# The last token tile's product in two column groups, each summed and stored when its own matmuls end

## The chip, the cores and the metric

The kernel runs on one core of a Trainium2 chip. The metric is the device time of one execution in microseconds (us). A run gives several executions; times of two kernels are compared within rounds taken on the same chip.

Names in the profiles: PE is TensorE (matmuls) and PEld its weight loads, DVE is VectorE, ACT ScalarE, POOL GpSimd and SP SyncE; a `q` after a name marks the engine's sequencer, which waits and issues DMAs. SBUF is the working memory; PSUM, in banks, is where matmuls sum up. A DMA has *landed* when the last update of its semaphore arrives.

A profile's *span* runs from its first to its last instruction. It is about 1.7 us shorter than the device time of the same execution (172.957 against 174.68 us for the kernel before).

## The reference, cut to what matters

Each of 2048 tokens (448 features) goes through a linear-attention block and a mixer-plus-MLP block in parallel. Both end in a matrix product, and their sum leaves the kernel:

```python
# x: 2048 x 448;  xn = layernorm(x)
# ... attention output o (2048 x 448), MLP hidden h3 (2048 x 1792), x1 = xn + mixer ...
out = x + (o @ wo) + (x1 + h3 @ w4)
```

The tokens are worked in 16 tiles of 128. For one tile, `h3 @ w4` takes 14 matmuls with a contraction of 128, and `o @ wo` takes 4 (here with padding to 128). All 18 accumulate in one PSUM bank. Then VectorE adds `xs`, which is `x + x1` of that tile, and the result is stored.

## The kernel before

Every operation is recorded first; waits are then worked out from what it reads and writes. Two rules of that matter here. SBUF is tracked in small pieces, but PSUM by whole bank: a matmul that writes a bank waits for every earlier reader on another engine of any column of that bank. And waits are placed mainly between different engines; in the last tile no matmul waits for an earlier matmul, so PE's own instructions simply follow each other.

```python
def _keys(self, ap):
    ...
    if psum:
        lo = (ap.offset * esz) % row_bytes
        hi = lo + esz + sum(step * (num - 1) for step, num in list(ap.ap)[1:]) * esz
        return [(name, b) for b in range(lo // 2048, (hi - 1) // 2048 + 1)]   # whole banks
    ...

def play(e, eng):                      # one engine's instructions
    mine = []
    for fn, todo, src, dma in self.stream[eng]:
        for f, i in todo:
            e.wait_ge(...)
        ins = fn(e)
        ...
    for f in mine:                     # at the end: wait for this engine's own stores
        if f not in self.marked:
            e.wait_ge(get(f), 16)
```

The end of the kernel:

```python
def x_sum(i):
    R.ew(pool, "tensor_tensor", xs[:, i % 2, :], xn[:, i, 0:D], xtok[:, i, :], op=ALU.add)

def fin_bank(i):
    return (0 if i > 13 else 4) + i % 2

def fin_full(i):
    g, j = divmod(i, 4)
    b = banks[fin_bank(i)]
    x_sum(i)
    for fc in range(FC):               # FC = 14
        R.mm(b[:, 0:D], h3T[:, g % 2, fc, 128 * j:128 * j + 128], w4[:, fc, :], fc == 0, False)
    for kc in range(KC):               # KC = 4
        R.mm(b[:, 0:D], oT[:, g % 2, kc, 128 * j:128 * j + 128], wo[:, kc, :], False, kc == KC - 1)

# ... all other tiles, in pairs ...
fin_full(14)
fin_out(14)                            # one add of 448 columns
store(14)
fin_full(15)
for h in range(2):
    c = slice(224 * h, 224 * h + 224)
    R.ew(dve, "tensor_tensor", outb[:, 3, c], banks[fin_bank(15)][:, c], xs[:, 1, c], op=ALU.add)
    R.dma(out2d[128 * 15:, c], outb[:, 3, c], "ACT" if h else "SP")
```

So before the change, the last tile is 18 matmuls of 448 columns, then two adds of 224 columns, each with its own store, the first issued by SP, the second by ACT.

The softmax here doesn't subtract the row's maximum and nothing guards it: scores larger than these inputs give would overflow.

## Time and profile before

| | before |
|---|---|
| device time, median of 3 (lowest to highest) | 174.75 us (174.6 to 175.1) |
| span of the profile | 173.0 us |
| PE busy | 168.8 us, 98% of the span |
| first matmul of the last tile | 166.63 us |
| last matmul of the last tile ends | about 170.2 us |
| from the first matmul of the last tile to the end of the span ("the tail") | 6.33 us |

Two lines of the profile's page say who is the bottleneck. The first gives each engine's busy time, its share of the span and its instruction count; the second the shares of the chain that ended last.

```profile
PE 168.8 (98%) x2254; PEld 90.0 (52%) x2254; DVE 114.2 (66%) x263; ACT 84.3 (49%) x99; POOL 88.7 (51%) x123
...
PE 97%; DVE 0%; ACT 0%; issue 0%; DVEq 0%
```

The last lines of that chain in order of time (start, duration, what) show PE without a break until 170.21 us. The chain does not follow a store to its landing, so its end is not the end of the span.

```profile
24.40 145.81 PE bank L200 x1924
170.21 0.02 issue
170.23 0.39 DVE vaug L212
170.62 0.30 DVEq L173
```

The timeline of the end (start, duration, engine, line, operation, out<-in, shape, count, and in brackets the idle time before and who ended it). `w,phik` are the operands of the MLP product, `wo,xnT` of the attention product, and the VectorE output tile goes by the name `vaug`, whose memory it reuses.

```profile
166.63 2.81 PE L200 MATMUL bank<-w,phik 128*128 128x448 bf16 x14
...
169.28 0.92 PE L200 MATMUL bank<-wo,xnT 128*128 128x448 bf16 x4
170.23 0.69 DVE L212 TENSOR_TENSOR vaug<-bank,vaug 128x224 bf16<-128x224 f32 x2 [2.78 <-PE bank L200]
170.95 0.36 ACTq L218 DMA_DIRECT2D out_dram<-vaug  x1
```

What to see: VectorE idles 2.78 us until PE's last matmul is done, then does *both* adds, and only then can ACT issue the last store. The view of DMA issues gives the median time from issue to landing in the last column:

```profile
out_dram<-vaug SPq DMA_DIRECT2D x15, 112.0 KB, 1.9
...
out_dram<-vaug SPq DMA_DIRECT2D x1, 56.0 KB, 1.5
out_dram<-vaug ACTq DMA_DIRECT2D x1, 56.0 KB, 1.6
```

170.95 + 1.6 us is about 172.55; about 0.4 us more pass until the span ends.

### The profile page before, as it was taken

How to read it: one execution, taken by the hardware profiler on the slowest of the kernel's cores; microseconds unless marked ns; L12 is line 12 of the kernel's file. 1: busy time of each engine (PE TensorE's matmuls, PEld its weight loads, DVE VectorE, ACT ScalarE, POOL GpSimd, SP SyncE). 2: the span in 40 equal slices, each digit the busy share in tenths (PEclk: the TensorE clock that was granted, in tenths of full speed). 3: DMA queues.
4: the chain of work that ended last, by engine and by line, in shares of the span. 5: the costliest groups of instructions: out<-in, count | busy, mean ns of one | idle time of the engine just before them, and what ended most of it. 6: DMA issues, size and time to landing. Idle time of an engine off the chain costs nothing.

```text
span 173.0 us, 5182 instructions
## 1 busy us (share of the span) xinstructions
PE 168.8 (98%) x2254; PEld 90.0 (52%) x2254; DVE 114.2 (66%) x263; ACT 84.3 (49%) x99; POOL 88.7 (51%) x123
## 2 busy tenths in 40 slices
PE   7999999999999999999999999999999999999993
PEld 5565576544555554554545555555545545545451
DVE  4999976277999999976678953436407434474711
ACT  3599874988778877947225222224213222224000
POOL 3065570015789999930749388540721705423740
PEclk9999999999999999999999999999999999999999
DMA  5996642129942011043103824035321210311331
GB/s 164 347 216 79 143 90 56 35 46 366 380 151 48 18 30 30 4 55 70 34 0 75 83 61 87 5 84 111 73 51 34 74 44 4 83 34 30 83 107 29
DMA packets 32678, 15.20 MB, mean 88 GB/s; under 512 B 24080, under 2 KB 32016, under 8 KB 32656
## 3 DMA queue, kind: packets, MB, share of 16 engines
q1 hardware_dynamic: 32096, 14.48, 35.2%
q10 hardware_dynamic: 560, 0.40, 0.8%
q8 instruction: 17, 0.28, 0.7%
q14 instruction: 5, 0.04, 0.1%
HBM read 7.14 MB, written 1.84 MB: 52 GB/s over the span
## 4 chain that ended last, share of the span: by engine, by line
PE 97%; DVE 0%; ACT 0%; issue 0%; DVEq 0%
PE bank L200 96%; PE bank L204 1%; ACT xnT L208 0%; DVE vaug L212 0%; DVEq L173 0%; DVE gT L212 0%
## 5 line engine op out<-in xcount | busy, mean ns | idle before, releaser
L208 ACT ACTIVATE phik<-bank 128x1024 bf16<-128x1024 f32 (+1 forms) x44 | 42.3, 984 | 60.3 <-PE bank L200 60.2
L200 PE MATMUL bank<-gT,w 64*128 64x512 bf16 x392 | 50.0, 377 | 0.0
L212 DVE TENSOR_TENSOR vaug<-bank,vaug 128x464 f32<-128x464 f32 (+3 forms) x65 | 32.6, 512 | 23.0 <-PE bank L200 21.4
L200 PE MATMUL bank<-w,phik 64*128 64x448 bf16 (+1 forms) x420 | 45.0, 349 | 0.0
L212 POOL TENSOR_TENSOR xnT<-vaug 128x196 bf16<-128x196 f32 (+1 forms) x32 | 18.0, 585 | 46.4 <-DVE vaug L212 46.4
L200 PEld LDWEIGHTS bank<-w,phik 64*128 64x128 bf16 (+1 forms) x420 | 21.7, 94 | 21.2 <-issue 0.4
L212 POOL TENSOR_TENSOR phik<-phik,rks 128x1792 bf16<-128x1792 bf16 x8 | 25.6, 3212 | 10.4 <-DVE rks L212 10.3
L200 PEld LDWEIGHTS bank<-gT,w 64*128 64x128 bf16 x392 | 17.6, 94 | 17.5 <-ACT phik L208 0.4
L212 POOL TENSOR_TENSOR vaug<-xn,xtok 128x448 f32<-128x448 bf16 x16 | 16.2, 1032 | 0.2 <-DVE vaug L212 0.2
L212 DVE TENSOR_REDUCE ksum<-phik 128x64 f32<-128x1792 bf16 x8 | 16.1, 2011 | 0.0
L212 DVE RECIPROCAL vaug<-bank 128x16 f32<-128x16 f32 x16 | 4.1, 256 | 18.0 <-PE bank L200 18.0
L200 PE MATMUL bank<-xnT,wpq 64*128 64x512 bf16 x112 | 14.7, 376 | 0.0
L200 PE MATMUL bank<-wv,xnT 64*128 64x448 bf16 x112 | 13.9, 351 | 0.1
L200 PE MATMUL bank<-wo,xnT 64*128 64x448 bf16 (+1 forms) x106 | 13.4, 349 | 0.0
L200 PE MATMUL bank<-xnT,w 64*128 64x512 bf16 (+2 forms) x168 | 13.3, 306 | 0.0
L200 PE MATMUL bank<-w,hT 64*128 64x448 bf16 x112 | 13.2, 349 | 0.0
L200 PE MATMUL bank<-wpk,xnT 64*128 64x448 bf16 x112 | 13.2, 349 | 0.0
L212 POOL TENSOR_TENSOR rs<-mv,mhalf 128x1 f32<-128x1 f32 (+2 forms) x16 | 10.8, 674 | 1.3
L212 DVE TENSOR_TENSOR xn<-bank,xn 128x512 bf16<-128x512 f32 (+1 forms) x16 | 9.2, 619 | 3.1 <-PE bank L200 3.1
L212 DVE BATCH_NORM_STATS2 st<-xtok 128x6 f32<-128x448 bf16 x16 | 9.8, 612 | 0.0
L212 POOL TENSOR_SCALAR mv<-mv 128x1 f32<-128x1 f32 (+2 forms) x16 | 3.8, 238 | 11.3 <-DVE mv L212 10.9
L212 DVE BATCH_NORM_STATS2 st<-xn 128x6 f32<-128x448 bf16 x16 | 9.2, 577 | 0.0
(67 smaller groups left out, 173.4 us busy)
## 6 DMA issues: line engine op xcount, KB each, us to landing
w<-in_B_w_dram SPq DMA_DIRECT2D x2, 896.0 KB, 5.9
out_dram<-vaug SPq DMA_DIRECT2D x15, 112.0 KB, 1.9
w<-in_B_w_dram SPq DMA_DIRECT2D x1, 1568.0 KB, 11.1
xtok<-in_A_x_dram SPq DMA_DIRECT2D x2, 448.0 KB, 5.7
xtok<-in_A_x_dram SPq DMA_DIRECT2D x2, 224.0 KB, 4.4
w<-in_B_w_dram SPq DMA_DIRECT2D x2, 224.0 KB, 4.6
wo<-in_A_wo_dram SPq DMA_DIRECT2D x2, 224.0 KB, 7.0
xtok<-in_A_x_dram SPq DMA_DIRECT2D x3, 112.0 KB, 2.6
```

Source lines behind the costliest of these rows:

```text
L200: self.op("PE", lambda e: e.matmul(out, lhsT, rhs, start=start, stop=stop, skip_group_check=True), [out], [lhsT, rhs], tile=self._tile(lhsT))
L204: self.op("PE", lambda e: e.transpose(out, in_, ident), [out], [in_, ident], tile=self._tile(in_))
L208: self.op("ACT", lambda e: e.activation(out, in_, func, **kw), [out], [in_] + aps)
L212: self.op(eng, lambda e: getattr(e, name)(out, *args, **kw), [out], aps)
```

## The change

The intent: let VectorE sum and store most of the last tile while PE still works on the rest, so that only a narrow add and a small store remain after PE's last matmul. The 448 columns are done as a group of 336 in bank 1, then a group of 112 in bank 2. `x_sum` moves out of `fin_full`; POOL's order of work stays the same.

```diff
-        def fin_full(i):
+        def fin_full(i, c0=0, c1=D, b=None):
             g, j = divmod(i, 4)
-            b = banks[fin_bank(i)]
-            x_sum(i)
+            b = banks[fin_bank(i) if b is None else b]
             for fc in range(FC):
-                R.mm(b[:, 0:D], h3T[...], w4[:, fc, :], fc == 0, False)
+                R.mm(b[:, c0:c1], h3T[...], w4[:, fc, c0:c1], fc == 0, False)
             for kc in range(KC):
-                R.mm(b[:, 0:D], oT[...], wo[:, kc, :], False, kc == KC - 1)
+                R.mm(b[:, c0:c1], oT[...], wo[:, kc, c0:c1], False, kc == KC - 1)
 ... (cut)
+        x_sum(14)
         fin_full(14)
         fin_out(14)
         store(14)
-        fin_full(15)
-        for h in range(2):
-            c = slice(224 * h, 224 * h + 224)
-            R.ew(dve, "tensor_tensor", outb[:, 3, c], banks[fin_bank(15)][:, c], xs[:, 1, c], op=ALU.add)
-            R.dma(out2d[128 * 15:, c], outb[:, 3, c], "ACT" if h else "SP")
+        x_sum(15)
+        for c0, c1, bk, eng in ((0, 336, 1, "SP"), (336, D, 2, "ACT")):
+            fin_full(15, c0, c1, bk)
+            R.ew(dve, "tensor_tensor", outb[:, 3, c0:c1], banks[bk][:, c0:c1], xs[:, 1, c0:c1], op=ALU.add)
+            R.dma(out2d[128 * 15:, c0:c1], outb[:, 3, c0:c1], eng)
```

More of the change, by code (lines that the diff above doesn't have):

```diff
@@ L731, in fin_bank @@
             return (0 if i > 13 else 4) + i % 2
-        def fin_full(i):
+        def fin_full(i, c0=0, c1=D, b=None):
             g, j = divmod(i, 4)
-            b = banks[fin_bank(i)]
-            x_sum(i)
+            b = banks[fin_bank(i) if b is None else b]
             for fc in range(FC):
-                R.mm(b[:, 0:D], h3T[:, g % 2, fc, 128 * j:128 * j + 128], w4[:, fc, :], fc == 0, False)
+                R.mm(b[:, c0:c1], h3T[:, g % 2, fc, 128 * j:128 * j + 128], w4[:, fc, c0:c1], fc == 0, False)
             for kc in range(KC):
-                R.mm(b[:, 0:D], oT[:, g % 2, kc, 128 * j:128 * j + 128], wo[:, kc, :], False, kc == KC - 1)
+                R.mm(b[:, c0:c1], oT[:, g % 2, kc, 128 * j:128 * j + 128], wo[:, kc, c0:c1], False, kc == KC - 1)
         def fin_pair(i):
```

## The prediction

> # Prediction
>
> **What bounds the kernel now.** TensorE: the page gives PE 98% of the 173.0 us span, and the chain of waits is 97% PE, unbroken from 24.4 to 170.2 us. The change touches only what comes after 166.6 us, the end of that chain. Read from the timeline:
>
> - The last tile's 18 matmuls (128x128 weights, 448 columns) run from 166.63 to about 170.20 us. From (3.57 - 0.353)/17 they start 189 ns apart, each shown 353 ns long.
> - Then VectorE does two adds of 128x224, 170.23 to 170.92 us (385 ns each, overlapping by some 80 ns). It waited 2.8 us for PE before.
> - ACT's queue issues the second half's store at 170.95; it lands about 1.6 us later (DMA issues, 56 KB); the span ends at 173.0.
>
> So 2.75 us of tail follow PE: 0.7 us of adds, 1.6 us of store, about 0.4 us of end.
>
> **What the change does.** Same products, now 18 matmuls of 336 columns into one bank, then 18 of 112 into another; 18 more matmuls and weight loads.
>
> 1. PE. [...] 189 ns at 448 columns, and about 28 ns per pair of row halves at 62 columns, where each matmul has its own weight load too, so loads hid even there. [...] 18 x (142.5 + 49.2) = 3.45 us against 18 x 189.2 = 3.41 us. PE ends about 0.045 us later. [...]
> 2. First add and store (336 columns): a line through the trace's two lengths (385 ns at 224, 613 ns at 448) gives about 500 ns, from about 169.4 to 169.9 us; the store (SP queue) lands about 171.6, hidden behind the second group and the last store.
> 3. Last add: 112 columns, about 270 ns by the same line, about 170.28 to 170.55 instead of 170.92: -0.37 us, PE's +0.045 included.
> 4. Last store: 28 KB in 224-byte rows instead of 56 KB in 448-byte rows. A full-row store took about 1.67 us, the half-row one 1.6; another halving is worth about -0.05 us. [...]
>
> Nothing else is on the path: POOL's sums of both tiles are done by 166.1 us and keep their order; the second group's bank was last read by the GELU of an earlier pair, long before.
>
> **Sum.** -0.37 - 0.05 = about -0.4 us: 174.75 to 174.33 us (-0.25%), inside the 2% band. Range 174.0 to 174.75. Chances: faster by over 2% 0.01, within 2% 0.98, slower by over 2% 0.01.
>
> **What the profile should show.** PE instructions 2254 to 2272. Matmul starts about 142 ns apart in the first group, 49 in the second; PE ends at 170.2 to 170.3 us. A 336-column add inside PE's busy time; a 112-column add of about 270 ns as VectorE's only work after PE. The last store issued by ACT at about 170.6; span about 172.5 us.
>
> **What would make it wrong.** 128-row weight loads that don't hide behind 49 ns matmuls [...]; 224-byte-row stores slower than 448-byte ones; a wait at the start of the second group; run-to-run spread (174.6 to 175.1) of the size of the gain.

The 142.5 ns at 336 columns and 49.2 ns at 112 in point 1 are my estimates; the line through the two spacings of the trace of before, 189.2 ns at 448 columns and 28 ns a pair at 62, gives 142.4 and 48.9 ns.

## The result, and the profile after

| | before | after |
|---|---|---|
| device time, median of 6 | 174.89 us (174.6 to 175.1) | 174.53 us (174.3 to 174.8) |
| ratio, with its 95% interval | | 0.9981 (0.9966 to 0.9995) |
| span of the profile | 173.0 us | 172.7 us |
| PE instructions | 2254 | 2272 |
| tail | 6.33 us | 5.86 us |

Before was timed again in the same rounds as after, so its median is of 6 here and of 3 above. A ratio is the mean time of one kernel's runs over the mean of the other's of the same rounds, so it is not quite the ratio of the medians. The time fell by 0.36 us in the medians, 0.2%, with an interval that just excludes no change.

PE's line of the page after the change:

```profile
PE 168.5 (98%) x2272; PEld 91.3 (53%) x2272; DVE 114.2 (66%) x263; ACT 84.4 (49%) x99; POOL 88.8 (51%) x123
```

The timeline of its end, in the columns of before:

```profile
166.83 2.16 PE L200 MATMUL bank<-w,phik 128*128 128x336 bf16 x14
...
168.83 0.73 PE L200 MATMUL bank<-wo,xnT 128*128 128x336 bf16 x4
...
169.40 0.85 PE L200 MATMUL bank<-w,phik 128*128 128x112 bf16 x14
169.60 0.51 DVE L212 TENSOR_TENSOR vaug<-bank,vaug 128x336 bf16<-128x336 f32 x1 [1.94 <-PE bank L200]
...
170.08 0.36 PE L200 MATMUL bank<-wo,xnT 128*128 128x112 bf16 x4
170.48 0.27 DVE L212 TENSOR_TENSOR vaug<-bank,vaug 128x112 bf16<-128x112 f32 x1 [0.38 <-PE bank L200]
170.79 0.36 ACTq L218 DMA_DIRECT2D out_dram<-vaug  x1
```

And its DMA issues:

```profile
out_dram<-vaug SPq DMA_DIRECT2D x1, 84.0 KB, 1.6
out_dram<-vaug ACTq DMA_DIRECT2D x1, 28.0 KB, 1.5
```

The 336-column add now runs inside PE's busy time, and one add of 0.27 us follows PE instead of a pair of 0.69 us. The matmuls of the second group start 49 ns apart: 14 of them fill 0.85 us, the last one shown 213 ns long, so (0.85 - 0.213)/13 = 49 ns.

**Cutting the tail into steps.** The runs of one kernel spread by half a microsecond and more, which is as much as the effect. But that spread comes before the last tile: its first matmul starts anywhere from 166.48 to 168.08 us in the profiles. From there on the profiles repeat to about 0.02 us. So the theory is tested on the tail. The trace's semaphore events and instruction starts cut it into five steps that add up to it:

| step, us | before | after | difference |
|---|---|---|---|
| PE: first matmul of the tile to the last group's sum ready | 3.583 | 3.627 | +0.044 |
| VectorE: from there to the last add done | 0.723 | 0.308 | -0.415 |
| hand-over to the last store's issue | 0.021 | 0.022 | 0 |
| last store: issue to landing | 1.598 | 1.493 | -0.105 |
| landing to the end of the span | 0.405 | 0.405 | 0 |
| tail | 6.330 | 5.855 | -0.475 |

The tail gained 0.475 us; in this pair of profiles 0.20 us of that was lost again by a later start of the last tile (166.83 against 166.63). The difference arises in one place, in code that the change doesn't touch: up to 81.3 us PE was 0.08 us ahead of before, from 81.5 us on it was 0.21 us behind. The view of the waits, for 81 to 82.5 us of after, has a pause of the weight loads there (total, times, longest) that the same window of before has not:

```profile
PEld bank L200 <- issue: 0.6, 1, 0.6
```

"issue" means that the profile shows nothing to wait for. The semaphore events show it: PE waits there for four transposing DMAs that feed the next token group, the last of which landed at 81.19 us in before and at 81.45 in after. In the other profiles it landed between 81.0 and 82.7 us.

### The profile page after: what moved, and what is told of

It is laid out like the page before. It is cut to its first block, busy times and chain, and to the rows that moved or that the text cites. A ratio compares the mean times of both kernels' runs of the same rounds, so it can differ in the third digit from the quotient of the medians.

```text
span 172.7 us, 5218 instructions
## 1 busy us (share of the span) xinstructions
PE 168.5 (98%) x2272; PEld 91.3 (53%) x2272; DVE 114.2 (66%) x263; ACT 84.4 (49%) x99; POOL 88.8 (51%) x123
## 4 chain that ended last, share of the span: by engine, by line
PE 95%; DVE 2%; issue 1%; ACT 0%
PE bank L200 94%; PE bank L204 1%; DVE vaug L212 1%; DVE st L212 1%; ACT xnT L208 0%; DVE xn L212 0%; DVE mv L212 0%; DVE gT L212 0%; DVE rs L212 0%; DVE epsb L212 0%
## 5 line engine op out<-in xcount | busy, mean ns | idle before, releaser
L200 PE MATMUL bank<-w,phik 64*128 64x448 bf16 (+3 forms) x434 | 45.2, 343 | 0.0
L200 PEld LDWEIGHTS bank<-w,phik 64*128 64x128 bf16 (+1 forms) x434 | 22.9, 94 | 20.3 <-issue 0.4
L200 PE MATMUL bank<-wo,xnT 64*128 64x448 bf16 (+3 forms) x110 | 13.6, 343 | 0.0
L212 POOL TENSOR_SCALAR g_tok<-xn,rs 128x512 bf16<-128x512 bf16 x12 | 9.1, 776 | 0.3
(67 smaller groups left out, 173.0 us busy)
```

Source lines behind the costliest of these rows:

```text
L200: self.op("PE", lambda e: e.matmul(out, lhsT, rhs, start=start, stop=stop, skip_group_check=True), [out], [lhsT, rhs], tile=self._tile(lhsT))
L212: self.op(eng, lambda e: getattr(e, name)(out, *args, **kw), [out], aps)
```

## The experiments

Twelve runs, five rounds each (one is the changed kernel unedited, one repeats e2); all gave correct results. **The theory**: the gain is a shorter add after PE and a smaller last store, less a small cost on PE; it needs the second bank; nothing else moved. **Rivals**: that it is chance; that the finer adds and stores alone bring it; that it comes from any early store, whichever group is last; that the bank doesn't matter.

All tails and their steps, read as above ("sum" is PE's step, "add" VectorE's, "store" from issue to landing, "end" from landing to the end of the span; hand-over is 0.02 in all):

| kernel | sum | add | store | end | tail | ratio to before (95%) |
|---|---|---|---|---|---|---|
| before | 3.583 | 0.723 | 1.598 | 0.405 | 6.330 | |
| after | 3.627 | 0.308 | 1.493 | 0.405 | 5.855 | 0.9981 (0.9966 to 0.9995) |
| e0_again | 3.626 | 0.310 | 1.480 | 0.410 | 5.847 | 0.9984 (0.9946 to 1.0022) |
| e1_onebank | 4.403 | 0.309 | 1.481 | 0.405 | 6.620 | 1.0032 (0.9998 to 1.0065) |
| e2_addsonly | 3.582 | 0.723 | 1.626 | 0.410 | 6.363 | 1.0027 (0.9987 to 1.0067) |
| e2_repeat | 3.581 | 0.724 | 1.610 | 0.405 | 6.342 | 1.0014 (0.9988 to 1.0040) |
| e3_order | 3.626 | 0.542 | 1.666 | 0.415 | 6.271 | 0.9998 (0.9966 to 1.0029) |
| e4_c64 | 3.628 | 0.259 | 1.602 | 0.404 | 5.914 | 0.9977 (0.9956 to 0.9997) |
| e5_half | 3.628 | 0.425 | 1.576 | 0.409 | 6.059 | 0.9987 (0.9968 to 1.0006) |
| e6_swap | 3.627 | 0.310 | 1.451 | 0.498 | 5.902 | 0.9976 (0.9951 to 1.0001) |
| e7_c32 | 3.783 | 0.284 | 1.732 | 0.404 | 6.223 | 0.9994 (0.9974 to 1.0013) |
| e8_three | 3.671 | 0.258 | 1.446 | 0.405 | 5.801 | 0.9985 (0.9958 to 1.0012) |
| e9_swaprev | 3.627 | 0.309 | 1.455 | 0.416 | 5.824 | 0.9977 (0.9955 to 0.9998) |
| e10_threerev | 3.672 | 0.259 | 1.410 | 0.421 | 5.779 | 0.9983 (0.9961 to 1.0006) |

### e0_again: the change unedited

No edit.

> The changed kernel itself, unedited, for the spread and to see which of its numbers are the same from profile to profile. 'Tail' is the time from the first matmul of the last tile to the end of the span: 6.33 us in the profile of before, 5.86 us in that of after. Theory (the gain is the shorter last add, -0.42 us, and the smaller last store, -0.10 us, less 0.04 us on PE, and is all in the tail): tail 5.86 us within 0.05, ratio about 0.997 to 0.998. Rival (the gain is chance, or sits in earlier stages): tail or ratio differ by more than 0.2 us from these.

Measured: tail 5.847 us, each step within 0.013 us of after's. The tail's gain is not chance. The times alone would not have shown that: one run in six took 175.79 us, and the interval includes 1.

### e1_onebank: both groups in one bank

```diff
-        for c0, c1, bk, eng in ((0, 336, 1, "SP"), (336, D, 2, "ACT")):
+        for c0, c1, bk, eng in ((0, 336, 1, "SP"), (336, D, 1, "ACT")):
```

> Both column groups in bank 1, everything else as in after. Theory: the second group may not write the bank before the first add (about 0.51 us) has read it, so PE stands still from the end of the first group until the add ends: about 0.8 us more, tail 5.86 + 0.8 = 6.65 us, slower than before by about 0.3 us. Rival (the two groups alone bring the gain, banks don't matter): tail 5.86 us.

Measured: tail 6.620 us. The timeline of its end shows PE standing still for VectorE between the groups:

```profile
169.00 0.73 PE L200 MATMUL bank<-wo,xnT 128*128 128x336 bf16 x4
169.77 0.51 DVE L212 TENSOR_TENSOR vaug<-bank,vaug 128x336 bf16<-128x336 f32 x1 [1.94 <-PE bank L200]
...
170.34 0.86 PE L200 MATMUL bank<-w,phik 128*128 128x112 bf16 x14 [0.60 <-DVE vaug L212]
```

PE's step grew by 0.776 us over after's, and the split turned from a gain of 0.475 into a loss of 0.29. Without the second bank the split is a loss. The wait is placed by the kernel's own bookkeeping, which goes by banks. No run here tried the overlap within one bank without the wait.

### e2_addsonly and e2_repeat: cut the adds and stores alone

Before's kernel with only this edit:

```diff
-            c = slice(224 * h, 224 * h + 224)
+            c = slice(336 * h, 336 + 112 * h)
```

> Before's 18 matmuls of 448 columns in one bank; only the two final adds and stores are cut at 336 instead of 224. Theory: both adds still follow PE's last matmul, together about 0.72 us as before; only the last store shrinks from 56 to 28 KB, -0.10 us: tail 6.22 us. Rival (a small last add and store are enough, the split of the matmuls does nothing): tail 5.8 to 5.9 us.

> e2 unedited. Its profile had a tail of 6.36 us, as before's, yet its runs were 0.7 us slower in the median; in the profile PE stood still 1.2 us at 27 us for a transposing DMA, in code that the edit doesn't touch. If that is chance: runs again within 0.3 us of before, tail 6.36 us. If it belongs to this kernel: slower by 0.5 us or more again, with that wait in the profile.

Measured: tails 6.363 and 6.342 us, so no gain at all. The adds behaved as expected (0.723 us together, as before). My expected 0.10 us from the smaller store was a miss: 28 KB took 1.61 to 1.63 us to land here, against 1.48 to 1.49 in after. The repeat's lines of the timeline and of the DMA issues:

```profile
170.47 0.69 DVE L212 TENSOR_TENSOR vaug<-bank,vaug 128x336 bf16<-128x336 f32 x2 [2.78 <-PE bank L200]
171.19 0.36 ACTq L218 DMA_DIRECT2D out_dram<-vaug  x1
...
out_dram<-vaug SPq DMA_DIRECT2D x1, 84.0 KB, 1.6
out_dram<-vaug ACTq DMA_DIRECT2D x1, 28.0 KB, 1.6
```

(The first line counts the 336- and the 112-column add together.) The 84 KB store was issued only 0.19 us ahead, and in the repeat's trace its packets (171.84 to 172.25 us) overlap those of the small store (172.09 to 172.36). That gave a new question, what a close store ahead costs, which e5 and e8 answer.

The first e2 was also 0.77 us slower than before in the medians (175.45 against 174.68), although its tail was only 0.03 longer. Its profile shows where: PE waited for a transposing DMA at 27 us, which no other profile shows. The line of the waits in that window:

```profile
PE bank L200 <- DMA xnT<-xn: 1.2, 1, 1.2
```

In the repeat's profile that wait is gone, so it does not belong to the kernel; yet its median was still 0.36 us above before's. That remainder stays open.

### e3_order: the narrow group first

```diff
-        for c0, c1, bk, eng in ((0, 336, 1, "SP"), (336, D, 2, "ACT")):
+        for c0, c1, bk, eng in ((0, 112, 1, "SP"), (112, D, 2, "ACT")):
```

> Same two groups on two banks, but the narrow one (112 columns) first and the wide one (336) last. Theory: PE +0.04 us; the last add is 336 columns, about 0.54 us with its hand-over against 0.72 us for before's two adds, -0.18; the last store is 84 KB, +0.05 to +0.1: tail 6.2 to 6.3 us, little under before's 6.33. Rival (the gain comes from starting an add and a store before PE has ended, whichever): tail about 5.9 us.

Measured: tail 6.271 us. One wide add and a large store follow PE:

```profile
170.71 0.51 DVE L212 TENSOR_TENSOR vaug<-bank,vaug 128x336 bf16<-128x336 f32 x1 [2.29 <-PE bank L200]
...
out_dram<-vaug ACTq DMA_DIRECT2D x1, 84.0 KB, 1.7
```

The same matmuls, bytes and banks in the other order keep 0.06 us of the gain of 0.475. What counts is the size of what is left after PE, not that an add and a store start early.

### e5_half: two equal groups, two banks

```diff
-        for c0, c1, bk, eng in ((0, 336, 1, "SP"), (336, D, 2, "ACT")):
+        for c0, c1, bk, eng in ((0, 224, 1, "SP"), (224, D, 2, "ACT")):
```

> Two groups of 224 columns on two banks. PE +0.04 us, last add 385 ns alone, about -0.30 us for before's pair of adds. It also tells why after's last store landed 0.10 us sooner than before's. Theory A (its size: 28 KB against 56): here 56 KB again, so 1.60 us from issue to landing, tail 6.07 us. Rival B (before's last store ran close behind another one, 0.3 us earlier, and the two got in each other's way): here the other store is long past, so about 1.50 us, tail 5.97 us.

Measured: tail 6.059 us; the last store, 56 KB again, took 1.576 us:

```profile
171.24 0.36 ACTq L218 DMA_DIRECT2D out_dram<-vaug  x1
...
out_dram<-vaug ACTq DMA_DIRECT2D x1, 56.0 KB, 1.6
```

Theory A's tail was 6.07 and B's 5.97, so A holds: of the 0.105 us that after's last store gained, 0.083 (1.576 - 1.493) is its size, and at most 0.022 (1.598 - 1.576) is that before's ran 0.30 us behind another one; the same step of e2 and its repeat differs by 0.016. The DMA packets in the traces agree: from the first to the end of the last they took 0.338 us in before, 0.329 in e5 and 0.256 in after, and those of before's two stores did not overlap (171.485 to 171.806 and 171.830 to 172.168 us). Size here means rows as well as bytes: every store has 128 rows, so a smaller one has shorter rows, and no run tells the two apart.

### e4_c64 and e7_c32: a narrower last group

```diff
-        for c0, c1, bk, eng in ((0, 336, 1, "SP"), (336, D, 2, "ACT")):
+        for c0, c1, bk, eng in ((0, 384, 1, "SP"), (384, D, 2, "ACT")):      # e4
+        for c0, c1, bk, eng in ((0, 416, 1, "SP"), (416, D, 2, "ACT")):      # e7
```

> Cut at 384 instead of 336: the last group has 64 columns. Theory: matmuls 29 ns apart in it [...], PE's total as in after; last add about 220 ns against 274, last store 14 KB, 0.03 to 0.05 us less: tail about 5.77 us against 5.85 for after. If weight loads of 128 rows need more than 29 ns each, the spacing shows it and the tail grows by 18 times the excess.

> Cut at 416: last group 32 columns[...]. Theory: the first add (416 columns, about 585 ns) now outlasts the second group (0.28 us), so the last add waits for VectorE and not for PE, and the tail is longer than after's: about 5.95 us. Rival (the narrower the last group the better): 5.7 us. [...]

(The last store of e4 is 16 KB, not 14: 128 rows of 64 values of 2 bytes.) Measured: tails 5.914 and 6.223 us, both longer than after's 5.855, and longer than I expected. The end of e4:

```profile
170.09 0.57 PE L200 MATMUL bank<-w,phik 128*128 128x64 bf16 x14
170.29 0.75 DVE L212 TENSOR_TENSOR vaug<-bank,vaug 128x384 bf16<-128x384 f32 x2 [2.30 <-PE bank L200]
...
171.07 0.36 ACTq L218 DMA_DIRECT2D out_dram<-vaug  x1
...
out_dram<-vaug SPq DMA_DIRECT2D x1, 96.0 KB, 1.6
out_dram<-vaug ACTq DMA_DIRECT2D x1, 16.0 KB, 1.6
```

In e4 PE and VectorE did as expected (matmuls 29 ns apart, on the line through after's 49.2 ns at 112 columns and 142.5 at 336; add step 0.05 us shorter). The loss is in the store: 16 KB took 1.602 us, because the 96 KB store had been issued only 0.20 us before it (e8 tests this). The lines of e7:

```profile
170.22 0.50 PE L200 MATMUL bank<-w,phik 128*128 128x32 bf16 x14
170.42 0.69 DVE L212 TENSOR_TENSOR vaug<-bank,vaug 128x416 bf16<-128x416 f32 x2 [2.54 <-PE bank L200]
...
out_dram<-vaug ACTq DMA_DIRECT2D x1, 8.0 KB, 1.7
```

In e7, three things went wrong. The matmuls of 32 columns start 25 ns apart, not 16 as the same line gives and as my estimate of 0.28 us for the group had it, which costs 18 x 9 ns = 0.16 us. The first add (592 ns) outlasts the second group, so VectorE is what the last add waits for. And the last store, 8 KB, 0.10 us behind 104 KB, took 1.732 us. The narrower group is not better without end.

### e8_three: narrow last group, but the store ahead kept small and early

```diff
-        for c0, c1, bk, eng in ((0, 336, 1, "SP"), (336, D, 2, "ACT")):
+        for c0, c1, bk, eng in ((0, 256, 1, "SP"), (256, 384, 2, "SP"), (384, D, 3, "ACT")):
```

> Three groups on three banks, 256, 128 and 64 columns; the first two stores by SP, the last by ACT. e4 showed the 64-column add 50 ns shorter but the last store 0.11 us slower, 0.2 us behind a 96 KB store. Theory (crowding of the two stores): here the store ahead is 32 KB and about 0.45 us earlier, so the last one (14 KB) lands in 1.45 to 1.50 us; PE +0.045 us against after, last add -0.05: tail 5.80 to 5.86 us, no better than after by more than 0.05. Rival (a store of 128-byte rows is slow in itself): 1.60 us again, tail 5.95 us.

Measured: tail 5.801 us. The last store is e4's, 16 KB in rows of 128 bytes from ACT. Its line in the timeline and the DMA issues:

```profile
170.75 0.22 DVE L212 TENSOR_TENSOR vaug<-bank,vaug 128x64 bf16<-128x64 f32 x1 [0.23 <-PE bank L200]
171.00 0.36 ACTq L218 DMA_DIRECT2D out_dram<-vaug  x1
...
out_dram<-vaug SPq DMA_DIRECT2D x1, 32.0 KB, 1.5
out_dram<-vaug ACTq DMA_DIRECT2D x1, 16.0 KB, 1.4
```

1.446 us, with 32 KB issued 0.46 us ahead, against 1.602 in e4. Rows of 128 bytes are not slow in themselves; the large store close ahead is what cost e4 its gain (its size and its closeness were changed together). The cost is not in moving the bytes: the packets of the small store took 0.23 us in both, but in e4 the first came 0.91 us after the issue (0.86 in e8) and the landing 0.46 us after the last (0.36 in e8).

### e6_swap, e9_swaprev and e10_threerev: which queue stores last

```diff
-        for c0, c1, bk, eng in ((0, 336, 1, "SP"), (336, D, 2, "ACT")):
+        for c0, c1, bk, eng in ((0, 336, 1, "ACT"), (336, D, 2, "SP")):      # e6, e9
+        for c0, c1, bk, eng in ((0, 256, 1, "ACT"), (256, 384, 2, "ACT"), (384, D, 3, "SP")):   # e10
-                for f in mine:
+                for f in reversed(mine):                                     # e9, e10
```

> As after, with the queues exchanged: first store by ACT, last store by SP. SP's stores show their first packet 0.03 to 0.04 us sooner after the issue than ACT's, but SP has more waits to work off after a landing (0.28 us to its last instruction against 0.18 for ACT in the profile of before). Theory: nothing gained, tail 5.85 to 5.95 us. Rival (the store's queue matters): 5.80 us or less.

> e6 (last store by SP) with the closing waits of each engine in reverse order of issue, so that SP has worked off the old ones before the last store lands. e6: 1.45 us from issue to landing against 1.49 for ACT, but 0.50 us from landing to the end against 0.40. Theory (the 0.1 us is the waits that SP executes after the landing): 0.42 us or less to the end, tail 5.82 us. Rival (it is SP itself): tail 5.90 us as in e6.

> Three groups as in e8, the first two stores by ACT, the last by SP, closing waits reversed as in e9: the gains of both if there are any, tail 5.75 to 5.80 us; ratio to before about 0.997, not to be told from after's by the times.

Measured: tails 5.902, 5.824 and 5.779 us. SP's last store lands 0.03 to 0.04 us sooner after its issue than ACT's (1.451 and 1.455 us in e6 and e9 against 1.493 and 1.480 in after and e0_again, 1.410 in e10 against 1.446 in e8), but in e6 the step from landing to end grew from 0.405 to 0.498 us: the kernel asks for the waits in order of issue, but in the built program's trace the wait for an older store, landed 5 us before, still stands behind the last store's. Reversed (e9), the last store's wait is SP's last, and the step is 0.416. e10 takes both gains and has the shortest tail, 0.08 us below after's. Its ratio to before, 0.9983, cannot be told from after's 0.9981. e9 and e10 beat the change in the tail only; no time here proves them better.

## Why the prediction was right

Forecast 174.33 us, range 174.0 to 174.75; measured 174.53. The total alone tests little: the range ends at the old time, the runs spread by as much as the gain, and before itself came out at 174.89 in the comparison against the 174.75 that the forecast started from. The tail tests the mechanism: forecast -0.42 us (-0.37 - 0.05), measured -0.475. Point by point:

- *PE's cost, +0.045 us.* Right: +0.044. My estimates were 142.5 and 49.2 ns; the trace of after has 142.5 and 49.2. The risk named, 128-row weight loads that don't hide, did not come: the spacing is 49.2 ns with a load for each matmul, and e4 has 29 ns at 64 columns, on the line through after's two spacings.
- *The first add hidden, about 500 ns.* Right: 508 ns, starting 0.2 us after PE began the second group and over about 0.38 us before the last add begins.
- *The last add, -0.37 us with PE's cost in.* Right: -0.415 + 0.044 = -0.371.
- *The last store, -0.05 us.* Right in sign, half in size: -0.105 in this pair, -0.118 with e0_again. This is the mis-sized term. I had taken the slope from a 112 KB store by SP and a 56 KB store by ACT, and SP's stores land 0.03 to 0.04 us sooner for the same size (e6 against after and e0), which hid part of the slope; also, from 84 to 112 KB SP's stores grew by only 0.04 us (1.627 to 1.665), from 28 to 84 by 0.18. From ACT alone, with no store issued less than 0.46 us ahead: 16 KB 1.446 us, 28 KB 1.48 to 1.49, 56 KB 1.576, 84 KB 1.666. That is (1666 - 1446)/68 = 3.2 ns per KB on top of about 1.4 us.
- *Second bank free, no wait at its start.* Right; e1 shows what it would have cost otherwise.
- *Run-to-run spread of the size of the gain.* Right, and it is the reason why the time fell by 0.36 us in the medians while the tail lost 0.475. The interval of the ratio, 0.0005 to 0.0034 of 174.9 us, is 0.09 to 0.59 us and holds both.

What stays open: on two of the three chips of the experiments, several kernels gained less in time (by the ratios) than in the tail, by up to 0.4 us (e2), while on the chip of e4 to e7 both agreed within 0.05 us. Each kernel's interval still holds the figure of its tail, so this may be no more than the spread. The profiles place the differences before the last tile, mostly in the first 8 us and at 81 to 83 us, in code that is the same in all. For the second place there is a lead. PE there works off four waits in two instructions, and their order differs from build to build: the two builds of e2, from the same source, have the last-landing DMA in the first instruction and in the second. PE's next matmul started 0.25 us after that landing in the one and 0.09 us in the other. (The bookkeeping keeps what an instruction reads in a set, so such an order need not repeat; that is argued from the code.) So a build may be some 0.1 us faster or slower by luck; one pair of profiles is all that says so. Whether this and the landing times explain the whole difference was not settled.

## What to carry to other kernels

The end of a kernel that is bound by one engine is a relay: what counts is the piece of work that every later engine still has to do after the bound engine stops, so give the last piece fewer columns, in a bank of its own (without one, PE's step was 0.776 us longer in e1). Choose its size by all runners together: it must last long enough to cover the add of the group before it (e7's 18 x 25 ns = 0.45 us did not cover an add of 592 ns), and the store of that group must be well ahead of the last store (96 KB issued 0.20 us ahead in e4 against 32 KB 0.46 us ahead in e8: 1.602 against 1.446 us to landing). When the gain is as small as the spread of the runs, compare the unchanging stretch of the traces step by step, not the total times.

## What the runs measured

- Matmul spacing, each matmul with its own 128-row weight load: 25 ns at 32 columns (e7), 29 at 64 (e4), 49.2 at 112 and 142.5 at 336 (after), 56 at 128 (e8), 189.2 at 448 (before). The line through 112 and 336 columns, 0.4165 ns a column plus 2.55 ns, gives 29.2 at 64, 55.9 at 128 and 189.1 at 448; at 32 it gives 15.9, 9 ns less than measured.
- VectorE's add of a PSUM operand (fp32) and an SBUF operand (fp32) to a bf16 result: 223 to 225 ns at 64 columns (e8, e10), 274 at 112 and 508 at 336 (after), 390 at 224 (the first of before's pair), 592 at 416 (e7), 624 at 448 (before). The line through 112 and 336 columns, 1.045 ns a column plus 157 ns, gives 224 at 64, 391 at 224, 592 at 416 and 625 at 448. An add that directly follows another is shown some 10 ns shorter (380 at 224 in before, 265 at 112 in e2, 181 at 32 in e7 against the line's 190).
- Stores close to each other: a 28 KB store 0.19 us behind one of 84 KB landed 0.12 to 0.15 us later (e2 and its repeat) than 0.66 us behind one (after, e0_again), and a 16 KB store 0.20 us behind 96 KB 0.16 us later (e4) than 0.46 us behind 32 KB (e8).
- Closing waits: one more wait behind the landing of the last store cost 0.08 us (0.498 against 0.416 us, e6 and e9).
